# Moving the decay factors of a chunked attention: a masked table made on the chip, a scaled q on GpSimd, and xt evicted by ScalarE

## Chip, cores and metric

One Trainium2 chip, one core of it. The metric is device microseconds of one execution, a median over runs. Engines: PE is TensorE (PEld its weight loads), DVE is VectorE, ACT is ScalarE, POOL is GpSimd, SP is SyncE, which only issues transfers here. A "q" behind an engine's name means its issuing side.

## What is computed

Attention with a decay per head, then two mixtures of experts (MoE), one behind the other, the second with a limit of tokens for each expert.

```python
# q, k, v: 2 x 8 heads x 768 x 64
gamma = 1.0 - 2.0 ** (-5.0 - np.arange(H))
for t in range(S):
    state = gamma[None, :, None, None] * state + np.einsum('bhd,bhe->bhde', k[:, :, t], v[:, :, t])
    y[:, :, t] = scale * np.einsum('bhd,bhde->bhe', q[:, :, t], state)
...
x = y.transpose(0, 2, 1, 3).reshape(B * S, H * D)      # 1536 x 512
# each MoE layer, 8 experts, F = 1024
logits = x @ w_gate
expert_idx = np.argmax(logits, axis=1)
out[mask] = gate_w[mask, None] * (np.maximum(xe @ w1[e], 0.0) @ w2[e])   # xe = x[mask], for each expert e
```

Layer 2 keeps at most `capacity` tokens for each expert, in their order.

## The kernel before

The 1536 tokens are 12 tiles of 128, numbered n; tile n is chunk n // 2 of the sequence n % 2. The loop over n in `fused` (lines 662 to 700) does the attention chunk by chunk, in a software pipeline: step n holds the scores of tile n, the rest of tile n−1 and the combination of tile n−2. Each engine works through its own instructions in the order in which the code issues them; waits between engines are semaphores. What a step issues, in this order, with the letters that stand in the rows:

- `a_scores(n)`: on PE the products sc of k and q (line 508); on DVE two products Am = sc × mask (line 510), which cut off later positions.
- `a_decay(n+1)`: vp, the values times a power of gamma by position (line 498), on POOL (on DVE for tile 1).
- `combine` for tile n−2 (`comb(n−2)`): cb on PE (line 1334), which turns xt so that tokens lie on partitions, and adds the logits; DVE sums the logits (lgb or row, line 1340), ACT copies the row (lines 1345, 1349) and issues its store to x1d in HBM (line 564).
- `a_past(n−1)`: q times the state of the earlier chunks, on PE into ot (line 542).
- `a_state(n)`: du on PE (line 524), wn = du + state on DVE (line 527), wm = wn times gamma to the 128 on POOL (line 529).
- `a_out(n−1)`: Am times vp on PE, added to ot (line 555); DVE evicts it as xt = ot × g, in two halves (line 557). g holds the scale and the power of gamma of the query's position.
- the transfers of tile n+3 (qb, kt, vk) on SP's queue, and for n under 7 a clearing store of x2d.

The scale by position is thus split: vp carries gamma to the (127 − s) for the key, g carries gamma to the (s − 127) for the query, and both the chunk's own scores and the past go through g at the end.

The routing of the first eight tiles goes in two batches of four, started at n = 5 and n = 9. `pick` finds the best expert (bm, bk, bmk, boh, lines 588 to 592), `rank` counts on PE and DVE, and `slots` builds tables bR of 128x256 (line 622) that `place` feeds to PE (line 630). At n = 10 an early gather of rows from x1d is issued by POOL (rows<-x1d,eig, line 347). The last four tiles are routed one by one (rR line 234, tbp line 243). Behind the loop stand the end of tile 11, products h with the first expert's weights (`ahead`, line 434), and layer 1 and layer 2.

Weights arrive as f32 pieces st (line 138) and are split into two parts: whi by ACT (`split_hi`, line 159) and wlo by DVE (`split_lo`, line 170); the first expert's first four pieces (whole, line 150) are used as they are.

The constants lie in one table cst of 1236 columns. It is loaded in three pieces, of 320, 228 and 70 KB, among the first tiles on SP's queue (lines 638, 640, 697). PE opens with 40 products warm on ones (line 464), which compute nothing that is used.

Of the kernel before, what the change touches and what calls it, by code (L numbers as in the profile page):

```python
# [10 lines left out]
F32 = mybir.dt.float32  # L11
# [7 lines left out]
P = 128  # L19
# [3 lines left out]
NT = N // P  # L23
# [11 lines left out]
WARM = 40  # L35
# [10 lines left out]
def _consts(capacity):  # L46
    gamma = 1.0 - 2.0 ** (-5.0 - np.arange(H, dtype=np.float64))
    s = np.arange(P, dtype=np.float64)
    parts = []

    def put(name, a):
        a = np.asarray(a, dtype=np.float32).reshape(P, -1)
        lo = sum(x.shape[1] for x in parts)
        _C[name] = (lo, lo + a.shape[1])
        parts.append(a)

    put("mask", (s[:, None] <= s[None, :]))
    put("dec", gamma[None, :] ** (127.0 - s[:, None]))
    hh = np.array([[2 * p + j for p in range(NP)] for j in range(2)]).repeat(HD, axis=0)
    put("g128", gamma[hh] ** 128.0)  # L60
    ho = np.array([[4 * a + 2 * u + j for j in range(2) for a in range(2)] for u in range(2)]).repeat(HD, axis=0)
    put("g", (1.0 / np.sqrt(HD)) * gamma[ho][:, :, None] ** (s[None, None, :] - 127.0))
    put("ident", np.eye(P))
    put("lt", (s[:, None] < s[None, :]))
    put("rev", np.broadcast_to(8.0 - np.arange(E), (P, E)))
    put("iota", np.broadcast_to(np.arange(C0), (P, C0)))
    put("tok", P * np.arange(NT)[None, :] + s[:, None])
    put("tie", np.broadcast_to((E - np.arange(E)) / 16, (P, E)))
    put("pos", np.broadcast_to(np.arange(E), (P, E)))
    put("slot", np.stack([s, s + P], axis=1))  # L70
    put("caps", np.broadcast_to(np.minimum(np.array(CAPS), [[N], [capacity]]).reshape(1, -1), (P, 2 * E)))
    put("held", np.broadcast_to(np.array(CAPS[1]), (P, E)))
    cand = np.arange(P) // NM
    put("cj", cand[:, None] == np.arange(E)[None, :])
    put("cbase", [[c[j] + (p % NM) * P if j < E else 2000 for c in CAPS] for p, j in enumerate(cand)])
    return np.ascontiguousarray(np.concatenate(parts, axis=1))


@with_exitstack
def fused(ctx, tc, qT, kT, vkr, wg, w11, w12, w21, w22, cst, out, capacity):  # L80
# [15 lines left out]
    c0, c1 = _C["g128"][1], _C["ident"][1]  # L96
# [9 lines left out]
    ident = con("ident")  # L106
# [364 lines left out]
    with tc.tile_pool(name="ap", bufs=3) as ap:  # L471
# [6 lines left out]
        st_, vps = {}, {}  # L478

        def a_load(n):  # L480
# [3 lines left out]
            qb = ap.tile([P, NP, P], F32, tag="qb", name="qb", bufs=4)  # L484
# [16 lines left out]
        def a_scores(n):  # L501
# [7 lines left out]
            for j in range(2):  # L509
                V.tensor_mul(Am[:, :, j, :], sc[j], con("mask").unsqueeze(1).to_broadcast([P, NP, P]))  # L510
# [22 lines left out]
        def a_past(n):  # L533
            c, b = divmod(n, B)
            qb = ld.pop(n)[0]
# [10 lines left out]
        def a_out(n, beside=None):  # L546
# [4 lines left out]
            for j in range(2):  # L551
                for a in range(2):
                    for u in range(2):
# [3 lines left out]
                V.tensor_mul(xt[:, 2 * j:2 * j + 2], ot[j],  # L557
                             con("g").rearrange("p (k t) -> p k t", k=KD)[:, 2 * j:2 * j + 2])
# [96 lines left out]
        first, second = (hi + 1 for _, hi in BATCHES)  # L655
        a_decay(0)
# [6 lines left out]
        for n in range(NT):  # L663
            a_scores(n)
            if n == NT - 1:
                split_lo()
# [26 lines left out]
            if n == 0:  # L693
# [185 lines left out]
    def layer(li, xd, rin):  # L879
# [29 lines left out]
        if li == 0:  # L909
            ix = finish_route(rin, li, [None, None, lambda: evac(0), None, None, done])  # L910
# [517 lines left out]
```

## Time and profile before

| | us |
|---|---|
| median of 3 runs | 422.79 (421.86 to 422.96) |
| the profiled execution: time | 423.04 |
| the profiled execution: span in the trace | 421.3 |
| PE busy in the span | 408.0 (97%) |
| DVE busy | 319.4 (76%) |
| ACT busy | 238.6 (57%) |
| POOL busy | 98.1 (23%) |

The busy times are sums over the whole span, and the stages differ: the attention takes roughly the first 62 us, the rest are the MoE layers. The rows below come from the windows (busy time in a stretch), from the timeline (each instruction or group with what ended the idle time ahead of it) and from the chain that ended last.

### The profile page before, as it was taken

To read this page: it belongs to the slowest core of one execution; us is meant where nothing else is said; L and a number is where in the kernel's file an instruction comes from. 1 tells how busy PE (TensorE), PEld (TensorE's weight loads), DVE (VectorE), ACT (ScalarE), POOL (GpSimd) and SP (SyncE) were. 2 spreads that over 40 slices of the span, in tenths; PEclk is the share of its full clock that TensorE was granted. 3 is DMA by queue.
4 is the path that set the end of the run, shared out by engine and by line. 5 is a ranking of instruction groups with operands and counts; after the bars stand their busy time and mean duration, and the time that the engine had idled before them with its cause. 6 is when DMAs were issued, how large, how long until landed. Compare 5 with 4: busy or idle time off the path is not lost.

```text
span 421.3 us, 9473 instructions
## 1 busy us (share of the span) xinstructions
PE 408.0 (97%) x3403; PEld 382.0 (91%) x3403; DVE 319.4 (76%) x870; ACT 238.6 (57%) x485; POOL 98.1 (23%) x89
## 2 busy tenths in 40 slices
PE   8998989999999999999999999999999999999993
PEld 7887779999899999999999988999888999999993
DVE  3778787678989798989798867378576788887840
ACT  2111132567677676767665631557776678787650
POOL 2344313303023130404000204003221504021021
PEclk9999999999999999999999999999999999999999
DMA  8999983976667766767657903768867777778711
GB/s 309 397 389 385 344 325 99 345 262 206 237 222 232 242 211 235 237 226 233 225 178 222 330 10 78 308 220 269 293 219 256 229 247 261 243 240 269 233 42 33
DMA packets 32503, 100.45 MB, mean 238 GB/s; under 512 B 4669, under 2 KB 5181, under 8 KB 32448
## 3 DMA queue, kind: packets, MB, share of 16 engines
q1 hardware_dynamic: 25488, 82.74, 57.5%
q0 software_dynamic: 4656, 13.00, 9.0%
q10 hardware_dynamic: 2304, 4.02, 2.6%
q8 instruction: 29, 0.48, 0.4%
q14 instruction: 26, 0.21, 0.2%
HBM read 87.01 MB, written 12.99 MB: 237 GB/s over the span
## 4 chain that ended last, share of the span: by engine, by line
PE 74%; DMA 11%; DVE 6%; issue 3%; ACT 2%; SPq 1%; POOL 1%; POOLq 0%; ACTq 0%; DVEq 0%
PE h L800 16%; PE y L844 16%; PE h L801 7%; PE y L845 7%; PE h L434 5%; DMA st<-w 5%; PE cb L1334 4%; DMA vk<-vkr 3%; PE o L859 3%; PE o L861 3%; PE o L860 3%; PE tp L362 2%; DVE wlo L170 2%; DMA whole<-w 2%; DMA x1d<-row 1%
## 5 line engine op out<-in xcount | busy, mean ns | idle before, releaser
L170 DVE TENSOR_TENSOR wlo<-st,whi 128x1024 fp32r<-128x1024 f32 x120 | 145.0, 1216 | 2.5 <-ACT whi L159 2.5
L159 ACT CAST whi<-st 128x1024 fp32r<-128x1024 f32 x120 | 125.1, 1045 | 29.0 <-DMA st<-w 28.6
L844 PE MATMUL y<-h,whi 128*128 128x416 f32 (+9 forms) x384 | 117.2, 369 | 0.0
L800 PE MATMUL h<-x,whi 128*128 128x416 f32 (+9 forms) x384 | 114.5, 365 | 0.0
L845 PE MATMUL y<-h,wlo 128*128 128x208 f32 (+9 forms) x384 | 96.9, 252 | 0.0
L801 PE MATMUL h<-x,wlo 128*128 128x208 f32 (+9 forms) x384 | 96.7, 252 | 0.0
L844 PEld LDWEIGHTS y<-h,whi 128*128 128x128 f32 x384 | 72.1, 188 | 2.9 <-DVE rro L232 0.6
L800 PEld LDWEIGHTS h<-x,whi 128*128 128x128 f32 x384 | 72.1, 188 | 2.1 <-issue 0.6
L801 PEld LDWEIGHTS h<-x,wlo 128*128 128x128 f32 x384 | 73.4, 191 | 0.1
L845 PEld LDWEIGHTS y<-h,wlo 128*128 128x128 f32 x384 | 73.3, 191 | 0.0
L321 POOL DMA_INDIRECT x2d<-row,is x16 | 17.1, 1071 | 118.5 <-ACT row L1347 88.7
L812 DVE SCALAR_TENSOR_TENSOR h<-hs,h 128x416 fp32r<-128x416 f32 (+9 forms) x48 | 26.9, 561 | 19.1 <-ACT h L811 18.5
L321 POOL DMA_INDIRECT out<-ob,is x14 | 14.9, 1068 | 110.8 <-ACT ob L865 108.4
L811 ACT ACTIVATE h<-hs 128x416 fp32r<-128x416 f32 (+9 forms) x48 | 25.1, 523 | 25.5 <-DVE hs L786 25.4
L786 DVE TENSOR_TENSOR hs<-h,hb 128x208 f32<-128x208 f32 (+9 forms) x96 | 29.6, 347 | 6.8 <-ACT hb L785 6.8
L434 PE MATMUL h<-x,whole 128*128 128x128 f32 (+1 forms) x256 | 30.5, 277 | 0.0
L785 ACT COPY hb<-h 128x208 f32<-128x208 f32 (+9 forms) x96 | 27.0, 318 | 5.9 <-PE h L801 5.8
L1345 ACT COPY row<-cb 128x512 f32<-128x512 f32 x11 | 6.5, 586 | 41.1 <-DVE lgb L1340 25.0
L434 PEld LDWEIGHTS h<-x,whole 128*128 128x128 f32 x256 | 29.3, 192 | 0.3 <-issue 0.2
L347 POOL DMA_INDIRECT rows<-x1d,igs x14 | 24.3, 1735 | 9.2 <-issue 4.7
L786 DVE TENSOR_TENSOR yt<-y,yb 128x208 f32<-128x208 f32 (+9 forms) x48 | 15.0, 352 | 14.2 <-ACT yb L785 14.2
L859 PE MATMUL o<-whi,h 128*128 128x512 f32 (+1 forms) x64 | 24.3, 379 | 0.0
(198 smaller groups left out, 613.6 us busy)
## 6 DMA issues: line engine op xcount, KB each, us to landing
st<-w SPq DMA_DIRECT2D x120, 512.0 KB, 4.3
vk<-vkr SPq DMA_DIRECT2D x11, 512.0 KB, 6.0
whole<-w SPq DMA_DIRECT2D x8, 512.0 KB, 7.1
x2d<-zero SPq DMA_DIRECT2D x12, 260.0 KB, 7.6
qb<-qT SPq DMA_DIRECT2D x12, 256.0 KB, 5.7
x1d<-row ACTq DMA_DIRECT2D x11, 260.0 KB, 5.8
kt<-kT SPq DMA_DIRECT2D x11, 256.0 KB, 5.7
vk<-vkr ACTq DMA_DIRECT2D x1, 512.0 KB, 4.6
```

The source lines that it names most:

```text
L159: A.copy(hi, st)
L170: V.tensor_sub(lo, st, hi)
L321: ins = nc.gpsimd.indirect_dma_start(dst.rearrange("n (i d) -> (n i) d", i=parts) if parts > 1 else dst[:, :], bass.IndirectOffsetOnAxis(a ...
L434: T.matmul(ps[:, j], w[:, k, j % 2 * P:(j % 2 + 1) * P], x[:, k], start=k == 0, stop=k == KD - 1, skip_group_check=True)
L785: A.copy(b, ps[:, 1, :])
L786: V.tensor_add(out, ps[:, 0, :], b)
L800: T.matmul(ps, hi[:, k, fs], x[:, k, :, :cap], start=k == 0, stop=False, skip_group_check=True)
L801: T.matmul(ps[:, 0, :], lo[:, k, fs], x[:, k, 0, :cap], start=False, stop=k == KD - 1, skip_group_check=True)
L812: V.scalar_tensor_tensor(h[:, sl, 1, :cap], s, 0.0, h[:, sl, 0, :cap], ALU.max, ALU.subtract)
L844: T.matmul(ps[i], hi[:, ds], h[:, f, :, :cap], start=f == 0, stop=False, skip_group_check=True)
L845: T.matmul(ps[i][:, 0, :], lo[:, ds], h[:, f, 0, :cap], start=False, stop=f == KF - 1, skip_group_check=True)
L859: T.matmul(p, h[:, f, 0, ts_], hi, start=f == 0, stop=False)
```

## The change

- Scores: the mask becomes a table m8 of two halves (one for each j, the head's place in its pair), mask times the query's power of gamma and the scale. Am = sc × m8, in two DVE products of the same size as before.
- Past: from chunk 1 on, POOL makes qg = qb × gq, 128x512, right behind `a_scores(n)` in the code and ahead of vp(n+1); `a_past` reads qg in qb's place.
- xt therefore needs no factor, and ACT copies it from PSUM (two halves of 128x256); DVE's product goes.
- The tables: a new input grow of 2x896 (7 KB) is loaded first on ACT's queue; three products gb on PE (2 rows against 128x512) spread its powers over the partitions; DVE multiplies two of them with the mask into m8, ACT copies the third to gq. They stand in the code ahead of the first scores (`a_factors`).
- mask, ident, lt and iota are made by POOL at the start (three selects and an iota), and cst shrinks to 84 columns, one load of 42 KB. DVE's casts of lt and iota go.
- 24 warm-up products instead of 40; qb in three buffers instead of four.
- The `split_lo` at the last step of the loop and the two `split_hi` at the last but one leave the attention; the two `split_hi` move into the routing of layer 1, and the `split` behind it does one wlo more.

```diff
-WARM = 40
+WARM = 24
...
-    put("mask", (s[:, None] <= s[None, :]))
...
-    put("g", (1.0 / np.sqrt(HD)) * gamma[ho][:, :, None] ** (s[None, None, :] - 127.0))
-    put("ident", np.eye(P))
-    put("lt", (s[:, None] < s[None, :]))
...
-    put("iota", np.broadcast_to(np.arange(C0), (P, C0)))
...
+def _grow():
+    gamma = 1.0 - 2.0 ** (-5.0 - np.arange(H, dtype=np.float64))
+    h = 2 * np.arange(NP)[None, :] + np.arange(2)[:, None]
+    left = (1.0 / np.sqrt(HD)) * gamma[h][:, :, None] ** (np.arange(P) - 127.0)
+    j = np.arange(2)[:, None]
+    picks = [np.broadcast_to(j == 0, (2, P)), np.broadcast_to(j == 1, (2, P)), j == np.arange(P)[None, :] // HD]
+    return np.ascontiguousarray(np.concatenate([left.reshape(2, -1)] + picks, axis=1).astype(np.float32))
...
+        nc.scalar.dma_start(gr, grow)
+        mask = ap.tile([P, NP, P], F32, tag="xt", name="mask", bufs=2)[:, 0, :]
+        for t, op in (mask, ALU.is_ge), (ident, ALU.is_equal), (lt16, ALU.is_gt):
+            G.affine_select(t, ones16, pattern=[[1, P]], compare_op=op, fill=0.0, base=0, channel_multiplier=-1)
+        G.iota(iota16, pattern=[[1, C0]], base=0, channel_multiplier=0, allow_small_or_imprecise_dtypes=True)
...
+        def a_factors():
+            for j in range(3):
+                gb = mmtile("gb")
+                at = (NP + j) * P
+                T.matmul(gb, gr[:, at:at + P], gr[:, 0:NP * P], start=True, stop=True)
+                if j < 2:
+                    V.tensor_mul(m8[:, j], gb.rearrange("p (a t) -> p a t", a=NP),
+                                 mask.unsqueeze(1).to_broadcast([P, NP, P]))
+                else:
+                    A.copy(gq, gb.rearrange("p (a t) -> p a t", a=NP))
+
+        def a_query(n):
+            if n // B:
+                qg = ap.tile([P, NP, P], F32, tag="qg", name="qg", bufs=2)
+                G.tensor_mul(qg, ld[n][0], gq)
+                qgs[n] = qg
...
-            qb = ap.tile([P, NP, P], F32, tag="qb", name="qb", bufs=4)
+            qb = ap.tile([P, NP, P], F32, tag="qb", name="qb", bufs=3)
...
-                V.tensor_mul(Am[:, :, j, :], sc[j], con("mask").unsqueeze(1).to_broadcast([P, NP, P]))
+                V.tensor_mul(Am[:, :, j, :], sc[j], m8[:, j])
...
-            qb = ld.pop(n)[0]
+            ld.pop(n)
+            qb = qgs.pop(n, None)
...
-                V.tensor_mul(xt[:, 2 * j:2 * j + 2], ot[j],
-                             con("g").rearrange("p (k t) -> p k t", k=KD)[:, 2 * j:2 * j + 2])
+                A.copy(xt[:, 2 * j:2 * j + 2], ot[j])
...
-        nc.sync.dma_start(cs[:, :c0], cst[:, :c0])
+        nc.sync.dma_start(cs, cst)
         a_load(1)
-        nc.sync.dma_start(cs[:, c0:c1], cst[:, c0:c1])
...
+        a_factors()
         a_decay(0)
...
             a_scores(n)
-            if n == NT - 1:
-                split_lo()
+            a_query(n)
             a_decay(n + 1)
...
-                nc.sync.dma_start(cs[:, c1:], cst[:, c1:])
-            if n == 2:
-                V.tensor_copy(lt16, con("lt"))
-                V.tensor_copy(iota16, con("iota"))
...
-            if n == NT - 2:
-                split_hi()
-                split_hi()
...
-            ix = finish_route(rin, li, [None, None, lambda: evac(0), None, None, done])
+            ix = finish_route(rin, li, [None, None, lambda: evac(0), split_hi, split_hi, done])
```

PE, from the last warm-up on, before (line, operation, output <- inputs, shape, and how many in a row):

```order
L464 MATMUL warm<-ones_78 128x128
L508 MATMUL sc<-qb,kt 128x128 x8
L524 MATMUL du<-vp,vk 64x64 x8
L508 MATMUL sc<-qb,kt 128x128 x8
L524 MATMUL du<-vp,vk 64x64 x8
L555 MATMUL ot<-Am,vp 64x128 x8
```

and after:

```order
L466 MATMUL warm<-ones_79 128x128
L494 MATMUL gb<-gr 128x512 x3
L535 MATMUL sc<-qb,kt 128x128 x8
L551 MATMUL du<-vp,vk 64x64 x8
L535 MATMUL sc<-qb,kt 128x128 x8
L551 MATMUL du<-vp,vk 64x64 x8
L583 MATMUL ot<-Am,vp 64x128 x8
```

The three products gb stand ahead of the first scores; what follows keeps its order.

POOL, from the last tiles of the attention to the early gather (eig are its row numbers), before:

```order
L498 TENSOR_TENSOR vp<-vk,cs 128x512
L529 TENSOR_TENSOR wm_734<-wn_732,cs 128x256
L498 TENSOR_TENSOR vp<-vk,cs 128x512
L529 TENSOR_TENSOR wm_834<-wn_832,cs 128x256
L498 TENSOR_TENSOR vp<-vk,cs 128x512
L347 DMA rows<-x1d,eig 128x520
L347 DMA rows<-x1d,ig_1186 112x520
```

and after:

```order
L556 TENSOR_TENSOR wm_747<-wn_745,cs 128x256
L504 TENSOR_TENSOR qg<-qb,gq 128x512
L525 TENSOR_TENSOR vp<-vk,cs 128x512
L556 TENSOR_TENSOR wm_849<-wn_847,cs 128x256
L504 TENSOR_TENSOR qg<-qb,gq 128x512
L525 TENSOR_TENSOR vp<-vk,cs 128x512
L349 DMA rows<-x1d,eig 128x520
L504 TENSOR_TENSOR qg<-qb,gq 128x512
L349 DMA rows<-x1d,ig_1199 112x520
```

A qg stands ahead of each vp, and the last one, for tile 11, behind the early gather.

DVE, behind the first batch's count (n = 7), before:

```order
L1340 TENSOR_REDUCE lgb<-cb 128x8
L611 TENSOR_TENSOR E_122<-boh,cs 128x32
L613 TENSOR_TENSOR bro<-brk,boh 128x32
L614 TENSOR_REDUCE r_123<-bro 128x4
L527 TENSOR_TENSOR wn_576<-du,wm_427 128x256
L622 TENSOR_SCALAR bR<-iota_79,r_123 128x256 x2
L557 TENSOR_TENSOR xt<-ot,cs 128x256 x2
L510 TENSOR_TENSOR Am<-sc,cs 128x4x128 x2
```

and after:

```order
L1359 TENSOR_REDUCE lgb<-cb 128x8
L638 TENSOR_TENSOR E_107<-boh,cs 128x32
L640 TENSOR_TENSOR bro<-brk,boh 128x32
L641 TENSOR_REDUCE r_108<-bro 128x4
L554 TENSOR_TENSOR wn_585<-du,wm_432 128x256
L649 TENSOR_SCALAR bR<-iota_80,r_108 128x256 x2
L537 TENSOR_TENSOR Am<-sc,m_133 128x4x128 x2
```

xt is gone from the row; it stands on ACT, behind the row copies and the store of the tile before.

## Rows read from the trace of the kernel before

**Rows 1.** Windows: stretch, length, busy (count) PE PEld DVE ACT POOL, clock, DMA, GB/s.

```profile
30.00:40.00 10.00, 8.51 (x147) 7.20 (x146) 9.32 (x31) 1.37 (x4) 3.27 (x4) 1.00 1.03 386
...
60.00:70.00 10.00, 9.40 (x90) 8.78 (x89) 7.75 (x51) 2.58 (x6) 1.00 (x1) 1.00 0.27 88
...
100.00:200.00 100.00, 99.99 (x720) 96.62 (x719) 90.01 (x255) 70.21 (x145) 27.65 (x19) 1.00 0.68 227
```

**Rows 2.** Timeline, opening: start, us, engine, line, operation, out<-in, shapes, count, [idle before <-releaser].

```profile
1.07 4.45 PE L464 MATMUL warm<-ones 128*128 128x128 f16 x40 [1.07 <-DVE ones L461]
...
5.45 1.59 PE L508 MATMUL sc<-qb,kt 64*128 64x128 f32 x16
...
5.87 1.04 POOL L498 TENSOR_TENSOR vp<-vk,cs 128x512 f32<-128x512 f32 x1 [5.41 <-DMA vk<-vkr]
...
7.59 1.16 PE L508 MATMUL sc<-qb,kt 64*128 64x128 f32 x16
...
8.65 0.69 DVE L498 TENSOR_TENSOR vp<-vk,cs 128x512 f32<-128x512 f32 x1 [0.28 <-DMA vk<-vkr]
```

**Rows 3.** Timeline, PE behind the attention: prices of products at the high clock.

```profile
70.50 1.50 PE L374 MATMUL tp<-ones 128*128 128x128 f16 x24
...
72.23 8.20 PE L434 MATMUL h<-x,whole 128*128 128x128 f32 x72
```

**Rows 4.** Chain that ended last, tiles 2 and 3: start, us, what, count.

```profile
8.70 7.86 DMA vk<-vkr
...
17.81 0.69 PE du L524 x16
18.50 0.88 PE ot L555 x16
19.37 1.09 PE sc L508 x16
20.46 1.12 PE cb L1334 x8
21.59 0.60 PE ot L542 x16
```

**Rows 5.** DMA view, 0 to 100: loads of constants, size, us from issue to landing.

```profile
cs<-cst SPq DMA_DIRECT2D x1, 320.0 KB, 5.0
...
cs<-cst SPq DMA_DIRECT2D x1, 228.0 KB, 6.0
```

**Rows 6.** Timeline, tiles 7 and 8: slot tables on DVE and PE's waits.

```profile
32.48 1.60 DVE L622 TENSOR_SCALAR bR<-iota,r 128x256 f16<-128x256 f16 x2
...
34.56 1.17 PE L1334 MATMUL cb<-iw,xt 128*128 128x136 f32 x8 [1.00 <-DVE xt L557]
...
39.51 1.17 PE L1334 MATMUL cb<-iw,xt 128*128 128x136 f32 x8 [0.49 <-DVE xt L557]
```

**Rows 7.** Timeline, DVE in the picks of the first and second batch.

```profile
28.58 0.68 DVE L589 TENSOR_TENSOR bk<-lgb,bm 128x32 f32<-128x32 f32 x1
...
47.96 0.19 DVE L589 TENSOR_TENSOR bk<-lgb,bm 128x32 f32<-128x32 f32 x1
...
48.63 0.85 DVE L592 TENSOR_TENSOR boh<-bk,bmk 128x32 f16<-128x32 f32 x1
```

**Rows 8.** Timeline, end of the attention: the early gather, and PE's wait for rR.

```profile
55.12 1.22 POOL L347 DMA_INDIRECT rows<-x1d,eig  x1 [5.69 <-DMA whole<-w]
...
58.10 0.20 PE L243 MATMUL tbp<-E,rR 128*128 128x8 f16 x2 [1.14 <-DVE rR L234]
```

**Rows 9.** Timeline, ACT: a row's last copy, its store's issue, a half-size copy.

```profile
26.70 0.20 ACT L1349 COPY row<-lgb 128x8 f32<-128x8 f32 x1
...
28.09 0.33 ACTq L564 DMA_DIRECT2D x1d<-row  x1
...
63.74 0.37 ACT L1379 COPY row<-cb 128x256 f32<-128x256 f32 x1 [0.40 <-DVE lg L1370]
```

**Rows 10.** Timeline, DVE's splits of weights behind the routing.

```profile
73.81 2.36 DVE L170 TENSOR_TENSOR wlo<-st,whi 128x1024 fp32r<-128x1024 f32 x2 [1.17 <-ACT whi L159]
```

More of the change, by code (lines that the diff above doesn't have):

```diff
@@ L60, in _consts @@
     put("g128", gamma[hh] ** 128.0)
-    ho = np.array([[4 * a + 2 * u + j for j in range(2) for a in range(2)] for u in range(2)]).repeat(HD, axis=0)
-    put("g", (1.0 / np.sqrt(HD)) * gamma[ho][:, :, None] ** (s[None, None, :] - 127.0))
-    put("ident", np.eye(P))
-    put("lt", (s[:, None] < s[None, :]))
     put("rev", np.broadcast_to(8.0 - np.arange(E), (P, E)))
-    put("iota", np.broadcast_to(np.arange(C0), (P, C0)))
     put("tok", P * np.arange(NT)[None, :] + s[:, None])
@@ L76, in _consts, with fused @@
     return np.ascontiguousarray(np.concatenate(parts, axis=1))
+def _grow():
[5 more added lines that the diff above has]
+    return np.ascontiguousarray(np.concatenate([left.reshape(2, -1)] + picks, axis=1).astype(np.float32))
 @with_exitstack
-def fused(ctx, tc, qT, kT, vkr, wg, w11, w12, w21, w22, cst, out, capacity):
+def fused(ctx, tc, qT, kT, vkr, wg, w11, w12, w21, w22, cst, grow, out, capacity):
     nc = tc.nc
@@ L95, in fused @@
     cs = cp.tile([P, cst.shape[1]], F32, name="cs")
-    c0, c1 = _C["g128"][1], _C["ident"][1]
     def con(name):
@@ L104, in fused @@
     wgs = cp.tile([P, 2, KD, E], F32, name="wgs")
-    ident = con("ident")
+    ident = cp.tile([P, P], F32, name="ident")
     lt16 = cp.tile([P, P], F16, name="lt16")
@@ L477, in fused @@
         ld = {}
-        st_, vps = {}, {}
+        st_, vps, qgs = {}, {}, {}
+        gr = ap.tile([P, NP, 2, P], F32, tag="Am", name="gr", bufs=2).rearrange("p a j t -> p (a j t)")[0:2, 0:(NP + 3) * P]
+        nc.scalar.dma_start(gr, grow)
[3 more added lines that the diff above has]
+        G.iota(iota16, pattern=[[1, C0]], base=0, channel_multiplier=0, allow_small_or_imprecise_dtypes=True)
+        m8 = ap.tile([P, 2, NP, P], F32, name="m8", bufs=1)
+        gq = ap.tile([P, NP, P], F32, name="gq", bufs=1)
+        def a_factors():
[13 more added lines that the diff above has]
+                qgs[n] = qg
         def a_load(n):
@@ L1416 @@
         "w21": t1(np.asarray(inputs["moe2_w1"])), "w22": t2(np.asarray(inputs["moe2_w2"])),
-        "cst": _consts(capacity),
+        "cst": _consts(capacity), "grow": _grow(),
     }
```

## The prediction, made before the changed kernel ran

> **What bounds the kernel now.** I read the windows first. TensorE (PE) is busy 99.99 of the 100 us from 100 to 200 [rows 1]: the two MoE layers are a fixed amount of matmul work. The edits lie ahead of that, in the attention (up to about 62 us) and in the routing behind it, so what they gain or lose there is carried to the end at its own size, unless something else is late at the hand-over. In the attention PE is not full: 8.51 of 10 us in 30 to 40, and 9.40 in 60 to 70 [rows 1]. These stretches and the first 18 us are where time can move.
>
> Second, the opening in the timeline: 40 warm-up matmuls from 1.07, 4.45 long, then the first scores sc(0), which take 1.59 where the next sc takes 1.16; GpSimd (POOL) begins its first vp at 5.87, after 5.41 idle that end with vk's arrival [rows 2]. The warm-ups take 4.45 ÷ 40 = 0.111 each, later matmuls of the same shape 1.50 ÷ 24 = 0.0625 [rows 3]. So although the clock column says 1.00, the durations say that TensorE opens at its lower level (1.2 GHz). It rises within sc(0): half pace for x us costs x/2, so 1.59 − 1.16 = 0.43 is 0.86 us of it, and the rise is at 5.45 + 0.86 = 6.3.
>
> Third, the chain of waits: the transfer of vk(3) ends at 8.70 + 7.86 = 16.56, vp follows, and du(3) starts at 17.81; from there PE's own rows follow one another [rows 4] and nothing else is late until the routing of the first batch.
>
> **Part 1, the opening (tables worked out by three products).** 24 warm-ups end at 1.07 + 24 × 0.111 = 3.7. Then three products gb (2 rows against 128x512 f32) stand ahead of sc(0). An f32 record of 128 columns takes 8.20 ÷ 72 = 0.114 at the high level [rows 3]; gb has four times the columns and two records, so 3 × 2 × 4 × 0.114 = 2.7 us, or 5.4 at the lower level. If the clock rises at 6.3 as it did, 2.6 us pass at half pace (1.3 of the work) and 1.4 are left: gb ends and sc(0) starts at 7.7 instead of 5.45. From sc(0) to du(3) PE has 4 sc, 3 du, 2 out, 2 cb and one past: 4 × 1.09 + 3 × 0.69 + 2 × 0.88 + 2 × 1.12 + 0.60 = 11.0 [rows 4]; before, 17.81 − 5.45 = 12.4 passed, the rest being the slow sc(0) and waits for vk. Those waits go: the loads of 320 and 228 KB no longer stand ahead of vk(3) [rows 5], and 561 kB at 386 GB/s [rows 1] are 1.45 us, so vk(3) lands at 15.1 and its vp ends at 16.2. du(3) comes at 7.7 + 11.0 = 18.7: **+0.9**. Bounds: with a rise at 4.7 gb ends at 6.9, and du(3) at 17.95 with 0.05 of hand-overs, +0.1; with one only after gb, at 9.1, du(3) is at 20.1, +2.3. On POOL, mask, ident, lt and iota now stand ahead of vp(0). No row shows such an operation; the nearest is vp, 1.04 [rows 2], with four times the columns of a mask: between nothing and 4 × 1.04 = 4.2, under 5.41 of idle time either way, so I take nothing. DVE's two products with the mask, as long as Am's, lie under gb and sc(0).
>
> **Part 2, tiles 7 and 8.** VectorE (DVE) was late there: it worked through the slot tables bR (1.60 for two) and only then xt, and PE's cb waited 1.00 and 0.49 for xt [rows 6]. xt now goes to ScalarE (ACT), which copies 128x256 in 0.37 [rows 9], two a tile, under the next sc (1.09): −1.49. Against it stands POOL's new qg, 128x512 like vp, so 1.04 each, ten of them. DVE's operations that read SBUF alone stretch while POOL has such an operation: bk took 0.68 at 28.58, beside a vp, and 0.19 at 47.96, with POOL idle; boh took 0.85 beside a vp [rows 7]. A hold is thus 0.5 to 0.66 of DVE's time. bR is already held once; with two POOL operations a tile I charge one more, +0.55. Part 2: **−0.95** (bounds −1.5, and 0, where three holds eat it).
>
> **Part 3, picking the second batch (tile 9).** This DVE chain (bk to boh) lies ahead of Am and out on the path; one hold is in it already [rows 7]. qg(9) runs just ahead of that vp, beside the first of these operations. It starts before they do, so I charge less than a whole hold of 0.5: **+0.4**; bounds 0 and +1.04, all of qg.
>
> **Part 4, the end of the attention.** A wlo and both xt leave DVE's queue ahead of the slot table rR, and PE's wait of 1.14 for it goes [rows 8]: tbp would start at 58.10 − 1.14 = 56.95 and past(11) right behind, at 57.1, where it was at 58.25. But past(11) now needs qg(11), which POOL does behind the issue of the early gather: 55.12 + 1.22 + 1.04 = 57.4. So −0.85. Of the 0.60 that PE idles in 60 to 70 [rows 1], 0.45 is waiting behind xt and ranks on DVE and goes. Part 4: **−1.3**, bounds −1.6 (qg in time) and −0.25 (qg behind one more operation of 1.04).
>
> A rule of the Trainium skill speaks against qg on POOL. vp took 1.04 on POOL and 0.69 on DVE [rows 2], 1.5 times. The Trainium skill's "GPSIMD Engine Reference", section "Engine selection", gives elementwise two-input work to VectorE and calls GpSimd about twice as slow. By it qg would take 2 × 0.69 = 1.38 (an estimate), ten of them 3.4 us more of POOL's time and qg(11) 0.34 later, which turns the sum below into −0.4. The trace's ratio is milder, and the sum goes by the trace.
>
> **Part 5, behind the attention.** The split of one weight piece moves from the attention into the first routing: two whi on ACT and one wlo more on DVE, where four now stand in a row. DVE idled 1.17 ahead of the last two of them, waiting for whi, and one takes 2.36 ÷ 2 = 1.18 [rows 10]: the gap takes it, and what follows keeps its time. **+0.2** for hand-overs; bounds 0 and +1.2, a wlo that finds no gap.
>
> At nothing: the casts of lt and iota that go (DVE waits for PE there, at tile 2); the three loads of constants that become one of 42 KB, beyond the 1.45 us above; qb in three buffers instead of four, whose load now waits for sc(n) and qg(n) of the same step, both done before SP comes to it, and if POOL were late by an operation, the load of two tiles ahead would be by as much, which du doesn't see.
>
> Sum: 0.9 − 0.95 + 0.4 − 1.3 + 0.2 = **−0.75**. The profiled execution took 423.04 us (span 421.3), 0.25 above the median of 422.79: 422.3 for it and **422.0** for the median. A measurement of this kernel can tell about 0.3% (1.27 us) from no change: below 421.5 is faster, above 424.1 slower.
>
> **The rivals.** A, the clock; slower. The warm-up is cut before the rise and followed by products that use 2 of 128 rows. If TensorE doesn't rise with these, but only once full work has run for a while, say at 12, gb ends at 9.1, and the 2.9 us from there do 1.45 of work: du(3) is 3.8 late instead of 0.9, and the time is 422.0 + 2.9 = 424.9. From a rise at 10.5 on it is slower. For it: only dense 128-row matmuls preceded the rise here. Against: at the rise itself sc ran, which uses 64 rows [rows 2], and PE has no more gaps now than then.
>
> B, POOL's additions hold nobody; faster. qg may fall where DVE reads PSUM (Am, wn, tbp); the stretched rows read SBUF alone [rows 7]. Then part 2 is −1.5, part 3 nothing and qg(11) in time: 0.9 − 1.5 − 1.6 + 0.2 = −2.0, or 420.8; with the early rise of part 1, 420.0. Against it: with two POOL operations a tile a hold finds DVE's routing twice as often.
>
> C, ACT's queue. xt stands behind the issue of the x1d store, and that issue came at 28.09 although its row was ready at 26.70 + 0.20 [rows 9]: it waits 1.2 for an older transfer. xt has about 0.7 to spare under sc. Where the store waits so long, cb comes 0.5 late; in three tiles that is 1.5: 423.5.
>
> D, POOL opens late. If the first of the masks takes long, vp(0), du(0) and Am(0) are late. du(0) is itself 2.25 later now, so the cover is 5.41 + 2.25 = 7.7; 2 us beyond it give 422.0 + 2 = 424.0. The Trainium skill's "GPSIMD Engine Reference", section "Instruction dispatch", has the first call of a freshly loaded kernel pay for code loading, about 6 us; no run here shows it.
>
> **How the numbers follow.** Forecast 0.42 (421.1 to 423.2), A 0.15, B 0.25, C 0.08, D 0.10. Faster: B but for 0.02, and a third of the forecast's chance, 0.37. Slower: A from 10.5 on, 0.11, and the far ends of C and D, 0.07: 0.18. Within 0.3%: the rest, 0.45. The range of 420.2 to 424.3 leaves out 0.1 of B and 0.1 of A and D.
>
> **What would show it.** In the profile of the changed kernel: sc(0) at 7.7 and du(3) at 18.7 (A: sc rows near 2 us long, beyond 9); cb of tiles 7 and 8 with no wait; bk and boh stretched beside qg and vp; past(11) near 57.4, released by qg; vp(0) soon after vk(0) lands, at 5.9 (D: later than 7.7). I am wrong if PE waits for ACT's xt, or if PE stands idle around 72 or 97, because then gains ahead of it don't carry.

## The result and the profile after

The changed kernel took 426.03 us (median of 4 runs, 424.28 to 426.21), the kernel before 422.33 in the runs beside it: a ratio of 1.0095 [1.0069, 1.0122]. It is slower by 3.7 us, where 422.0 was forecast and the range ended at 424.3.

The profile that belongs to this result is of the 424.28 execution, 1.8 below the other three. Its page says (span, then busy time and count by engine):

```profile
span 422.5 us, 9477 instructions
...
PE 410.3 (97%) x3393; PEld 382.9 (91%) x3393; DVE 314.6 (74%) x846; ACT 247.9 (59%) x510; POOL 110.0 (26%) x103
```

DVE gave up 5 us, ACT took 9 and POOL 12, as the change says. PE is 2 us busier than before, 410.3 to 408.0. Where those lie, the timeline of the opening tells (start, us, engine, line, operation, count, [idle before <-releaser]):

```profile
1.14 2.74 PE L466 MATMUL warm<-ones 128*128 128x128 f16 x24 [1.14 <-DVE ones L463]
...
3.81 2.84 PE L494 MATMUL gb<-gr 2*128 2x512 f32 x6
...
6.58 1.55 PE L535 MATMUL sc<-qb,kt 64*128 64x128 f32 x16
...
8.91 1.04 POOL L525 TENSOR_TENSOR vp<-vk,cs 128x512 f32<-128x512 f32 x1 [6.65 <-DMA vk<-vkr]
...
10.01 1.12 PE L551 MATMUL du<-vp,vk 128*64 128x64 f32 x16 [1.88 <-POOL vp L525]
...
11.06 2.08 PE L535 MATMUL sc<-qb,kt 64*128 64x128 f32 x16
```

and the windows of PE there (stretch, length, busy, granted clock, DMA share, GB/s):

```profile
6.00:7.00 1.00, 1.00 (x8) 1.00 0.98 324
7.00:8.00 1.00, 1.00 (x14) 0.60 0.93 337
8.00:9.00 1.00, 0.13 (x2) 0.50 1.04 406
...
13.00:14.00 1.00, 1.00 (x20) 0.50 0.86 215
14.00:15.00 1.00, 1.00 (x21) 0.99 0.99 389
```

gb ran at the high level (2.84, where 2.7 was worked out for it), then the clock was granted at half from about 7.2 to 14.0, from the middle of sc(0) on. vk(0) landed 3 us later than before, so PE idled 1.88 ahead of du(0). sc(1) takes 2.08, where the row of before that answers to it has 1.16 [rows 2]. From 15 on nothing of this is left, and the loss of the opening is made. du(3) is at 21.60, where it was at 17.81 [rows 4].

Two further profiles of the same kernel, taken later (below, again2 and again3), took another course. This is the opening of again2, an execution of 425.92:

```profile
3.81 5.48 PE L494 MATMUL gb<-gr 2*128 2x512 f32 x6
...
9.22 2.08 PE L535 MATMUL sc<-qb,kt 64*128 64x128 f32 x16
11.22 1.12 PE L551 MATMUL du<-vp,vk 128*64 128x64 f32 x16
12.28 2.08 PE L535 MATMUL sc<-qb,kt 64*128 64x128 f32 x16
...
14.29 1.12 PE L551 MATMUL du<-vp,vk 128*64 128x64 f32 x16
15.19 1.23 PE L583 MATMUL ot<-Am,vp 128*64 128x128 f32 x16
16.35 1.26 PE L535 MATMUL sc<-qb,kt 64*128 64x128 f32 x16
```

Here the lower level lasts from the warm-ups through gb (5.48, twice 2.7), two rounds of scores and du(1), until about 15; the clock column says 1.00 all that time, as it did over the slow warm-ups of the kernel before, so only the durations show it. This is rival A.

Start times of the same groups on PE show where each part of the change went. Each is the start in the timeline, in us; "last ob" is ACT's last eviction of layer 2.

| | before | before2 | after | again | again2 | again3 |
|---|---|---|---|---|---|---|
| time of the execution | 423.04 | 422.97 | 424.28 | 422.96 | 425.92 | 424.99 |
| sc(0) | 5.45 | 5.13 | 6.58 | 6.82 | 9.22 | 9.22 |
| sc(4) | 19.30 | 19.88 | 23.09 | 20.70 | 24.46 | 23.07 |
| sc(6) | 27.91 | 28.48 | 31.70 | 29.31 | 33.07 | 31.96 |
| sc(9) | 42.98 | 43.09 | 45.19 | 42.99 | 46.57 | 45.46 |
| sc(11) | 52.75 | 52.73 | 55.48 | 53.29 | 56.86 | 55.77 |
| first h | 63.78 | 64.39 | 65.62 | 63.93 | 67.46 | 66.51 |
| h x72 | 72.23 | 72.84 | 74.49 | 72.82 | 76.34 | 75.39 |
| last ob | 414.26 | 413.62 | 416.21 | 415.09 | 418.06 | 416.70 |

For again2 against before: +5.16 up to sc(4), −1.05 from there to h x72 (51.88 instead of 52.93), −0.31 from h x72 to the last ob, +3.80 in all; what follows the last ob took 0.9 less, and the span is 2.9 longer. The opening lost 1.4 to 5.2 in the four profiles of the changed kernel, and from sc(4) to h x72 each of them was 0.6 to 1.5 shorter than the kernel before. Two things stand against calling that a gain of the change. A late opening alone does the same: before_gb below, which has none of the rest of the change, took 51.86 from sc(4) to h x72, as again2 did (51.88). And from h x72 to the last ob the two profiles of the kernel before differ by 1.25 (342.03 and 340.78; the changed kernel 341.31 to 342.27), so that a difference of 1 cannot be followed to the end.

### The profile page after: what moved, and what is told of

It is laid out like the page before. It is cut to its first block, busy times and chain, and to the rows that moved or that the text cites. A ratio compares the mean times of both kernels' runs of the same rounds, so it can differ in the third digit from the quotient of the medians.

```text
span 422.5 us, 9477 instructions
## 1 busy us (share of the span) xinstructions
PE 410.3 (97%) x3393; PEld 382.9 (91%) x3393; DVE 314.6 (74%) x846; ACT 247.9 (59%) x510; POOL 110.0 (26%) x103
## 4 chain that ended last, share of the span: by engine, by line
PE 92%; DVE 2%; issue 2%; DMA 2%; POOL 1%; ACTq 0%; POOLq 0%; ACT 0%; DVEq 0%
PE y L863 19%; PE h L819 18%; PE y L864 8%; PE h L820 8%; PE h L436 6%; PE cb L1353 6%; PE sc L535 3%; PE o L878 3%; PE o L880 3%; PE o L879 3%; PE tp L364 3%; PE ot L583 2%; PE du L551 2%; DMA vk<-vkr 2%; PE ot L570 1%
## 5 line engine op out<-in xcount | busy, mean ns | idle before, releaser
L831 DVE SCALAR_TENSOR_TENSOR h<-hs,h 128x416 fp32r<-128x416 f32 (+9 forms) x48 | 26.9, 561 | 19.3 <-ACT h L830 18.7
L878 PE MATMUL o<-whi,h 128*128 128x512 f32 (+1 forms) x64 | 24.3, 379 | 0.0
L880 PE MATMUL o<-whi,h 128*128 128x512 f32 (+1 forms) x64 | 23.5, 366 | 0.0
```

Of the source, the lines that this page charges most:

```text
L878: T.matmul(p, h[:, f, 0, ts_], hi, start=f == 0, stop=False)
L880: T.matmul(p, h[:, f, 1, ts_], hi, start=False, stop=f == KF - 1)
```

## The experiments

Each is the changed kernel with the edit shown, unless it says otherwise. Ratios are to the kernel before, run beside it.

**again, again2, again3**: no edit.

> The changed kernel once more, for a second profile of its opening. In the first one vk(0), whose issue stood behind gr and kt(0) on ScalarE's queue, landed at 8.8 instead of 5.8, PE idled 1.88 ahead of du(0), and the clock was granted at half from 7.2 to 14.0; du(3) came at 21.6, 3.8 later than before. Theory Q (queue): the late landing is a result of the order of the loads and comes again, with du(0) at about 10. Theory C (chance): it was one execution's, and vk(0) lands near 6 here; then du(0) follows sc(0) at about 8.1. Both: 424 to 426.5.

> The changed kernel again, for one more profile: both profiled executions so far (424.28 and 422.96) were its fast ones, while most of its times lie near 426.2. Theory A: in the usual execution the clock stays at half through gb and the first scores, as in vk0_on_sp and before_gb: gb 5.4 to 5.5 long, sc(0) at 9.2, sc(4) at 23.3 to 23.7, time 426. Rival F (it rises ahead of gb and falls behind it, as in the two profiles): gb 2.8 to 3.1, half clock from 7.2 on, time 423 to 424.5, and then the 426 comes from elsewhere (a fall near 58 to 62).

> As again2, a further profile of the same kernel: theory A gives gb of 5.4 to 5.5 us and sc(4) at 23.3 to 23.7 with 426; rival F gives gb of 2.8 to 3.1 and a half clock behind it.

again: 426.62, ratio 1.0075 [1.0055, 1.0096]; its profiled execution took 422.96. vp(0) began at 6.67 there, when vk(0) had landed, and PE did not wait ahead of du(0), so the 1.88 of idle time was one execution's: theory C. The clock fell behind gb again (half from 7.7 to 11.2), and sc(4) was 1.4 late. again2 (425.92) and again3 (424.99) both show gb at 5.48 and sc(0) at 9.22: theory A. In both, vk(0) was in time for du(0). So the late rise goes with the two profiles that lie nearer the usual time, and the fall behind gb with the two shorter executions; four profiles are too few to say how often each comes, and none of them is of an execution of 426.0 to 426.9, where six executions without a profile lie. Their mean granted clock is 0.993 to 0.996, that of again2 0.997, and that of the two with a fall behind gb 0.989 and 0.991: this speaks for the late rise in them, but does not show it (again3 has 0.991 for a fall at 58).

**before2**: the kernel before.

> The kernel before, for a second profile of its opening. If its opening depends on chance as the changed kernel's does, the first scores take 1.1 to 2.1 and sc(4) comes between 19.0 and 20.5; the clock does not fall behind sc(0), since no work with few rows stands there. Time 420 to 424.

422.97. sc(0) took 1.16 from 5.13 on, sc(4) came at 19.88. With the scores right behind 40 warm-ups the opening moves by 0.6 between the two profiles, not by 4.

**vk0_on_sp**

```diff
-            (nc.scalar if n == 0 else nc.sync).dma_start(vk, vkr[b, c])
+            nc.sync.dma_start(vk, vkr[b, c])
```

> The changed kernel with one edit: vk(0) is issued by SP right behind qb(0), not by ScalarE behind gr and kt(0). Theory Q: vk(0) lands at about 5.5, du(0) follows sc(0) at 8.1 without the 1.9 of idle time. If the low clock came from that idle time, du(3) is at 19.2 or earlier and the time 2 to 2.5 below the changed kernel's. Theory G (the low clock follows the three 2-row products, whatever comes behind them): the clock is at half from about 7 again, du(3) at 20 or later and the gain at most 1.9. If vk(0) was not what PE waited for, no change.

426.27, 1.0081 [1.0063, 1.0098]. vk(0)'s product vp(0) ran at 5.97, but gb took 5.48, sc(0) stood at 9.22 and sc(4) at 23.62. The transfer was not what the time hung on: with vk(0) early the kernel lost as much.

**warm40**

```diff
-WARM = 24
+WARM = 40
```

> The changed kernel with 40 warm-up products as before instead of 24. The warm-ups then end at 4 to 5.5, gb at 7 to 8.2, sc(0) starts there, 1 to 1.6 later than in the changed kernel, and du(0) still waits for vk(0) at about 10. Theory G: the clock falls behind gb as it did, for as long: du(3) at 21.6 to 23, time equal to the changed kernel's or up to 1.5 more. Theory W (too short a warm-up lets the clock fall): no half clock behind gb, du(3) at 19.6 to 20, 2 less than the changed kernel.

426.14, 1.0071 [1.0046, 1.0097]. The profile has the rise inside the warm-ups (40 took 3.65), gb at the high level but for its end (3.07), and then the fall: half clock from 7.2 to 14.0, sc(0), sc(1) 2.08 each, sc(4) at 23.06. The clock was high ahead of gb and fell all the same. Theory W falls.

**before_gb**: the kernel before, with grow loaded, 24 warm-ups and the three products.

```diff
-WARM = 40
+WARM = 24
...
+        for j in range(3):
+            gb = mmtile("gb")
+            at = (NP + j) * P
+            T.matmul(gb, gr[:, at:at + P], gr[:, 0:NP * P], start=True, stop=True)
         a_decay(0)
```

> The kernel before with one part of the change alone: grow loaded, 24 warm-ups and the three products gb ahead of sc(0), their results unused. Theory R: the clock rises late or falls behind gb, sc(4) comes 2.5 to 4 later than in the kernel before (at 21.8 to 23.3 instead of 19.3), and the time is 2.5 to 4 more. My first sum (gb costs its duration, and the clock rises as before): sc(4) at 20.2, +0.9.

425.80, 1.0103 [1.0044, 1.0162]: this one part alone costs what the whole change costs. It takes the 24 warm-ups along; no run has them without the products, but with 40 (warm40) the loss was the same. Its opening in the timeline:

```profile
3.74 5.49 PE L670 MATMUL gb<-gr 2*128 2x512 f32 x6
...
9.15 2.08 PE L519 MATMUL sc<-qb,kt 64*128 64x128 f32 x16
11.16 1.12 PE L535 MATMUL du<-vp,vk 128*64 128x64 f32 x16
12.21 1.67 PE L519 MATMUL sc<-qb,kt 64*128 64x128 f32 x16
```

sc(4) came at 23.31, 4.0 later than before, not 0.9. From there to h x72 it took 51.86, the kernel before 52.93: PE's waits for xt in tiles 7 and 8 were nothing and 0.22, although VectorE still evicts xt. The kernel before first, then before_gb:

```profile
32.39 1.04 POOL L498 TENSOR_TENSOR vp<-vk,cs 128x512 f32<-128x512 f32 x1 [2.60 <-DMA vk<-vkr]
...
35.05 1.04 POOL L509 TENSOR_TENSOR vp<-vk,cs 128x512 f32<-128x512 f32 x1 [2.70 <-PE brk L620]
...
36.07 0.86 DVE L633 TENSOR_SCALAR bR<-iota,r 128x256 f16<-128x256 f16 x2
...
37.51 1.19 PE L1349 MATMUL cb<-iw,xt 128*128 128x136 f32 x8
...
42.21 1.17 PE L1349 MATMUL cb<-iw,xt 128*128 128x136 f32 x8 [0.22 <-DVE xt L568]
```

In the kernel before, vp waited for vk's transfer and ran beside bR [rows 6]. In before_gb, where PE is later, vp no longer waits for the transfer and ends as bR begins.

**rows128**: vk0_on_sp, and grow padded with zeros to 128 rows, so that gb uses all rows at the same columns.

```diff
-    return np.ascontiguousarray(np.concatenate([left.reshape(2, -1)] + picks, axis=1).astype(np.float32))
+    a = np.concatenate([left.reshape(2, -1)] + picks, axis=1).astype(np.float32)
+    return np.ascontiguousarray(np.concatenate([a, np.zeros((P - 2, a.shape[1]), np.float32)]))
```

> vk0_on_sp with the three products gb over 128 rows: grow is padded with 126 rows of zeros (458 KB instead of 7), the same results at the same number of columns. Theory R (products that use 2 of 128 rows do not raise the clock, or let it fall): with 128 rows gb runs at or reaches the high level, no half clock behind it, sc(0) at 6.8 to 7.5, sc(4) at 20 to 20.8 instead of 23.6, and the time about 3 below vk0_on_sp, near 423. Theory L (any f32 product of 512 columns does it, whatever its rows): sc(4) at 23 or later, as in vk0_on_sp, and the time 426.

```profile
5.64 4.66 PE L495 MATMUL gb<-gr 128*128 128x512 f32 x6 [1.77 <-DMA gr<-grow]
...
10.23 1.16 PE L536 MATMUL sc<-qb,kt 64*128 64x128 f32 x16
```

With 128 rows the clock rose within gb (4.66 lies between 2.7 and 5.4), sc(0) ran at the high level, and no half clock came behind it. For the course of the clock in this profile that is theory R. The time did not follow, 425.96, 1.0082 [1.0048, 1.0117]: the load of 448 KB made gb wait 1.77, sc(0) stood at 10.23 and sc(4) at 23.00. As the course also differs between profiles of one kernel, one profile is a hint that the rows matter, and does not show it; as a remedy the experiment is none.

**gb_f16**: vk0_on_sp with grow as two f16 terms in 4 rows, one pass for each product, and 40 warm-ups.

```diff
+    hi = left.astype(np.float16)
+    lo = ((left - hi) * 4096).astype(np.float16)
+    rows = [np.concatenate([hi, picks], axis=1), np.concatenate([lo, picks / 4096], axis=1)]
```

> vk0_on_sp with grow in f16 (two terms, 4 rows) and 40 warm-ups: gb takes one pass of 512 columns for each product, 0.65 in all at the high level and 1.3 at the lower one, a quarter of the f32 products' time. Theory R with time (the clock falls because some 3 us or more of work with few rows stand in the opening): no half clock behind gb, sc(0) at 5.5 to 6.8, sc(4) at 18.8 to 19.8, and the time 2.0 to 1.2 below the kernel before, 421 to 421.8, since what follows sc(4) gains 1.5. If even so short a stretch lets the clock fall: sc(4) at 21 or later and 423 or more.

423.62, 1.0041 [1.0013, 1.0069]: 2.4 less than the changed kernel, still above the kernel before. gb took 0.82, no half clock followed, sc(4) came at 19.67. From there to h x72 it took 52.52, only 0.4 less than before; a wait of cb for xt in step 6 is new. The lines of ACT and PE there:

```profile
26.65 0.59 ACT L1368 COPY row<-cb 128x512 f32<-128x512 f32 x1 [1.23 <-DVE lgb L1363]
27.13 0.20 ACT L1372 COPY row<-lgb 128x8 f32<-128x8 f32 x1
...
29.58 0.33 ACTq L595 DMA_DIRECT2D x1d<-row  x1
29.95 0.65 ACT L589 COPY xt<-ot 128x256 f32<-128x256 f32 x2 [2.62 <-PE sc L539]
30.38 1.19 PE L1357 MATMUL cb<-iw,xt 128*128 128x136 f32 x8 [0.81 <-ACT xt L589]
```

The row was ready at 27.33, its store was issued at 29.58, and xt stood behind it: rival C, of which the changed kernel's own profiles show at most 0.21 (again3). Waits of 0.3 and more for ScalarE's xt are only in versions whose sc(4) comes by 21.1.

**gb_f16_q11**: gb_f16 with the last qg ahead of the early gather.

```diff
+                a_query(NT - 1)
                 early(rt1, x1d, nb * P)
```

> gb_f16 with the last qg (tile 11) moved ahead of the early gather on GpSimd, one tile earlier. In the changed kernel it ran from 58.51 to 59.79 and VectorE's E (1.17 instead of 0.22) was held beside it, so that PE waited 0.83 for rR. Theory H (the hold): E takes 0.22 again, past(11) comes 0.6 to 0.9 earlier against sc(11), and the first h 0.3 to 0.9 earlier; time 0.3 to 0.9 below gb_f16. Rival: the gather is issued 1.3 later, and its rows are late for tp: no gain, or a loss up to 0.5.

423.99, 1.0033 [0.9994, 1.0072], no gain. In the profile E took 0.22 again, as theory H has it, and PE waited neither for rR nor for the gather's rows, so the rival did not come. Yet sc(11) to the first h took 10.71, gb_f16 10.23: the clock was granted at half from 54.6 to 58.1, with PE busy all that time. The opening took another course too, though its work is that of gb_f16: gb took 1.46, sc(0) 2.08, and sc(4) came at 20.78. A late rise thus comes behind 40 warm-ups and 4-row f16 products as well.

**f32_behind**: 40 warm-ups, and the f32 products behind sc(0).

```diff
                     T.matmul(sc[j][:, p, :], kt[hs, p, :], qb[hs, p, :], start=True, stop=True)
+            if n == 0:
+                a_factors()
```

> The changed kernel with 40 warm-ups and the three f32 products gb behind sc(0) instead of ahead of it. Theory P (the place: whatever stands ahead of the scores while the clock is low costs up to twice, and the scores raise the clock): sc(0) at 4.8 to 5.5 as in the kernel before, sc(4) at 20 to 21 instead of 23.1. Theory R in full (2-row products let the clock fall wherever they stand): half clock behind gb again, sc(4) at 22 to 23.5, no gain.

In the profile (425.08) sc(0) came at 5.09, gb took 2.84, no half clock followed, sc(4) stood at 20.93: theory P for that execution. The time is 426.56, 1.0083 [1.0056, 1.011], and the mean granted clock of its other executions lies at 0.982 to 0.995, mostly below the 0.993 of the profiled one. What they did is not in a profile.

**f16_behind** (gb_f16 with the products behind sc(0)) and **store_behind** (that, with the store's issue behind the next xt):

```diff
-            a_store(n, row)
+            if n < NT - 2:
+                stores.append((n, row))
...
                 a_out(n - 1)
+            while stores:
+                a_store(*stores.pop(0))
```

> gb_f16 with the products gb behind sc(0): sc(0) follows the 40 warm-ups as in the kernel before and gb takes 0.65 to 1.3 there, under the wait for vp. sc(4) at 18.5 to 19.3 (19.30 before, 19.67 in gb_f16). What is left is then the x1d store: in gb_f16 its issue waited until 29.58 and xt stood behind it, so that cb waited 0.81. That wait comes here too, as large or larger (0.8 to 1.5), and the time stays within 0.5 of gb_f16 or 0.5 below it: 422.5 to 423.5.

> f16_behind with the issue of each x1d store moved on ScalarE's queue behind xt of the next tile. If the store's wait is what held xt and cb: no wait of cb for xt, sc(7) to sc(8) unchanged, the time 0.8 to 1.5 below f16_behind and 0.5 to 1.5 below the kernel before. Rival: the wait for the transfers only moves, to vk and so to vp and du, or the store comes late for the early gather: no gain over f16_behind.

424.72, 1.0027 [0.9991, 1.0063], and 426.02, 1.0063 [1.0041, 1.0086]. In f16_behind's profile the clock fell behind gb once more (0.50 from 9 to 11), though gb took only 0.82; sc(4) came at 21.08, not at 18.5 to 19.3. In store_behind cb no longer waits for xt, and sc(9) stands at 42.18, 0.8 earlier than in the kernel before. It loses at the end of the attention: rR stands beside qg and takes 2.24, and the clock falls behind the stretch where PE has gaps (columns as in rows 1):

```profile
56.06 2.24 DVE L240 TENSOR_SCALAR rR<-iota,r 128x256 f16<-128x256 f16 x1
56.93 1.27 POOL L508 TENSOR_TENSOR qg<-qb,gq 128x512 f32<-128x512 f32 x1
...
58.36 0.20 PE L249 MATMUL tbp<-E,rR 128*128 128x8 f16 x2 [1.84 <-DVE rR L240]
```

```profile
54.00:58.00 4.00, 2.51 (x41) 1.94 (x39) 3.91 (x10) 1.23 (x3) 2.32 (x2) 1.00 0.98 347
58.00:62.00 4.00, 3.64 (x34) 2.96 (x35) 1.79 (x11) 0.37 (x1) 0.21 (x1) 0.58 0.37 130
```

The same fall is in again3 (0.71 from 58 to 62), gb_f16_q11, xt_dve and qg_dve, and in neither profile of the kernel before.

**qg_dve**: store_behind with qg on VectorE.

```diff
-                G.tensor_mul(qg, ld[n][0], gq)
+                V.tensor_mul(qg, ld[n][0], gq)
```

> store_behind with qg made by VectorE (0.69 each, by vp's row) instead of GpSimd. Theory H (holds): the stretched rows beside qg go (bk 0.19 again where no vp runs), sc(10) to sc(11) shrinks from 5.98 by 0 to 0.5, and past(11) no longer waits behind a held E; against it stand 0.69 in each tile on VectorE, which shows in tiles 7, 9 and 11, where VectorE is late: net between 0.6 faster and 1.0 slower than store_behind. The rule that elementwise work of two inputs belongs on VectorE would give the fast end.

427.60, 1.0111 [1.0082, 1.0141]; the profiled execution took 422.68. In it sc(10) to sc(11) is 5.27 instead of 5.98: the hold of the second pick is gone (boh 0.19). But the early gather came late (tp waited 1.36 for its rows), and the clock fell from 62 on. In its profile the placing of qg is worth 0.7 of a tile. Three executions without a profile took 427.45 to 428.09, longer than any of store_behind's, at a mean granted clock of 0.982 to 0.987 where the profiled one has 0.992; what they did is not known.

**xt_dve**

```diff
-                A.copy(xt[:, 2 * j:2 * j + 2], ot[j])
+                V.tensor_copy(xt[:, 2 * j:2 * j + 2], ot[j])
```

> The changed kernel with xt copied by VectorE as before (without a factor), not by ScalarE. It measures parts 2 and 4 of the prediction. If moving xt is what took PE's waits of 1.00 and 0.49 in tiles 7 and 8 away, they come back, longer by a hold or two of the doubled GpSimd work: 1.5 to 2.5 slower than the changed kernel by sc(9), and another 0.5 to 0.8 at the end of the attention. If those waits went because of something else (slot tables earlier), the same time within 0.5.

426.95, 1.0086 [1.0061, 1.0111]. PE's waits for xt in tiles 7 and 8 came back, 0.66 and 0.22, and sc(4) to sc(11) took 34.19 instead of 32.39, +1.8. With qg on GpSimd, moving xt to ScalarE is worth that much there. The whole times (ratios 1.0086 and 1.0095) do not tell the two apart.

**tables_loaded**: 40 warm-ups, no products; m8 and gq come ready-made (512 and 256 KB).

```diff
+        nc.sync.dma_start(m8.rearrange("p j a t -> p (j a t)"), grow[:, 0:2 * NP * P])
         a_load(1)
+        nc.sync.dma_start(gq.rearrange("p a t -> p (a t)"), grow[:, 2 * NP * P:])
```

> The changed kernel without the products gb: m8 and gq are loaded ready-made (512 and 256 KB, where the kernel before loaded 320 and 228 KB), 40 warm-ups, the rest as changed. Theory O (the loss is the opening's, made by gb's place and rows): sc(0) at 5.1 to 5.5, no half clock behind it, 220 KB more than before are 0.6 us of transfers, so sc(4) at 19.5 to 20.3, and the 1.5 gained behind sc(4) is kept: the time is between 1.2 below and 0.3 above the kernel before. Rival S (the rest of the change loses too in most executions, by a clock that falls near the end of the attention or by stores on ScalarE's queue): 1 to 2.5 above it.

The profiled execution took 422.63, with sc(0) at 5.51 and no half clock; sc(4) came at 20.52, since sc(1) waited 1.09 for kt, and from sc(4) to h x72 it took 52.06 instead of 52.93. Over all its executions the median is 424.92, 1.0063 [1.004, 1.0087], so theory O holds for the opening and not for the time, which lies 2.7 above the kernel before, just beyond rival S's 1 to 2.5. cb waited 0.58 for xt behind a store in it too. Of the executions at 424 to 426 there is no profile.

## Why the prediction was wrong

**The step that failed** is in part 1: "If the clock rises at 6.3 as it did". The prediction carried the rise of the kernel before over to an opening with other work in it. The price by either level was right: gb took 2.84 and 5.48, where 2.7 and 5.4 were worked out. The course of the clock was not. It either stayed low until about 12 to 15 (again2, again3, vk0_on_sp, before_gb) or rose ahead of gb and fell behind it for 3 to 7 us (after, again, warm40). The part was put at +0.9, with +2.3 for its far end; measured at sc(4) it was +1.4 to +5.2, and before_gb shows +4.0 for it alone. The far end was wrong too: it let the clock be high from the end of gb, and in again2 sc(0), du(0), sc(1) and du(1) stood at half as well.

**Rival A** had this mechanism, with its point (a rise after 10.5 makes the kernel slower) and a price of 424.9 for a rise at 12. again3, with the rise in sc(1), had du(3) at 21.58, 3.8 late as rival A worked out, and took 424.99; again2, with a rise near 15, 425.92. It was given 0.15, because sc, which uses 64 rows, ran at the rise of the kernel before. That argument looked at the work at the moment of the rise, and not at the 4.45 us of 128-row products ahead of it. The range ended below both. That the few rows are what delays the rise is argued, not shown: rows128 is for it, and in f32_behind's profile the same 2-row products behind sc(0) went without a fall, so that the place may matter as well.

**The early landing of vk(3)**, −1.45 of transfers, did come: in again vp(3) ran at 14.86, before at 16.72. It was worth nothing, as PE was later than that in every profile.

**Part 2** came out larger than forecast, but not by its mechanism alone: sc(6) to sc(9) took 13.49 in the profile after, 15.07 before, −1.58, and −1.4 to −1.6 in the others; forecast −0.95. The lines of tiles 7 and 8, against [rows 6]:

```profile
36.04 0.86 DVE L649 TENSOR_SCALAR bR<-iota,r 128x256 f16<-128x256 f16 x2
...
36.78 1.27 POOL L504 TENSOR_TENSOR qg<-qb,gq 128x512 f32<-128x512 f32 x1
37.28 1.19 PE L1353 MATMUL cb<-iw,xt 128*128 128x136 f32 x8
...
41.69 1.19 PE L1353 MATMUL cb<-iw,xt 128*128 128x136 f32 x8
```

cb waits for nothing, and bR ran clear of POOL's operations, 0.86 instead of 1.60: the hold that I charged did not come, and the old one went too. Against before2, where the waits of cb were 1.0 together, the gain of this stretch is 1.1. But before_gb, with xt on VectorE and no qg, took 13.76: the late opening removes most of these waits by itself, and against it the rest of the change gains 0.3 here. Where the opening is earlier and no store holds xt, the gain stands: f32_behind (sc(4) at 20.93) and store_behind (20.07) took 13.50.

**Part 3** was right: sc(9) to sc(11) took 10.29, before 9.77, +0.5 for the +0.4. The rows that answer to [rows 7] are held beside qg and vp:

```profile
49.36 0.61 DVE L616 TENSOR_TENSOR bk<-lgb,bm 128x32 f32<-128x32 f32 x1
...
49.89 1.26 POOL L504 TENSOR_TENSOR qg<-qb,gq 128x512 f32<-128x512 f32 x1
50.01 1.19 DVE L617 TENSOR_TENSOR bk<-bk,cs 128x32 f32<-128x32 f32 x1
...
51.11 1.04 POOL L525 TENSOR_TENSOR vp<-vk,cs 128x512 f32<-128x512 f32 x1
...
51.45 0.75 DVE L619 TENSOR_TENSOR boh<-bk,bmk 128x32 f16<-128x32 f32 x1
```

**Part 4** had the wait of [rows 8] in the wrong place. past(11) did not wait for qg(11) but still for rR, since qg(11) held E on DVE:

```profile
58.51 1.28 POOL L504 TENSOR_TENSOR qg<-qb,gq 128x512 f32<-128x512 f32 x1
...
58.66 1.17 DVE L227 TENSOR_SCALAR E<-roh,cs 128x8 f16<-128x8 f16 x1
...
60.36 0.20 PE L245 MATMUL tbp<-E,rR 128*128 128x8 f16 x2 [0.83 <-DVE rR L236]
```

0.83 of the 1.14 are left (1.3 in again2). sc(11) to the first h took 10.14 to 10.74 instead of 11.03: −0.3 to −0.9, forecast −1.3 (before2 took 11.66). The 0.45 of idle time between 60 and 70 was misread: the timeline of before has two waits of 0.30 there, both put down to DMA:

```profile
61.63 0.63 PE L377 MATMUL tp<-cs,rows 128*128 128x128 f32 x4 [0.30 <-DMA rows<-x1d,eig]
...
63.68 0.20 PE L243 MATMUL tbp<-E,rR 128*128 128x8 f16 x2 [0.30 <-DMA x1d<-row]
```

In before2 the second is put down to rR. The changed kernel has a new one of 0.36, of cb for E. **Part 5**: the first h to h x72 took 8.87 instead of 8.45, +0.4 for the +0.2. That is not the moved split but a wait for the last tile's routing on DVE, which the kernel before has in neither profile:

```profile
67.14 0.17 PE L225 MATMUL rk<-roh,lt 128*128 128x8 f16 x1 [0.39 <-DVE roh L213]
```

Behind the start of h x72 some profiles have a second wait, and it is the prediction's own sign of being wrong, PE idle around 72. In again, ACT's copy x came 2.1 after the start of the products tp that it reads, where it came 0.4 after them in the profile after:

```profile
72.43 0.55 PE L379 MATMUL tp<-ident,rows 112*128 112x112 f32 x4
...
74.53 0.59 ACT L380 COPY x<-tp 128x224 f32<-128x224 f32 x2 [3.39 <-PE h L436]
...
74.93 7.40 PE L436 MATMUL h<-x,whole 128*128 128x112 f32 x64 [1.05 <-ACT x L380]
```

The same wait, 0.93 to 1.01, is in vk0_on_sp, warm40, xt_dve, f32_behind, f16_behind, store_behind and qg_dve, and in none of the three with the two `split_hi` where the kernel before has them (before, before2, before_gb). Seven profiles with the moved `split_hi` lack it too, so the move does not explain it by itself; what held ACT is not shown.

**The size of qg** was read off vp, at 1.04. It took 1.27: vp's second input is one column for each head, qg's is as long as the first. The Trainium skill's "GPSIMD Engine Reference", section "Engine selection", had given about 1.38 (an estimate) by twice VectorE's time; VectorE made the same qg in 0.68 in qg_dve, 1.27 is 1.9 times that, and the trace agrees with the page better than with the row that I took.

**Rival B** came in part 2 only (no hold at bR); DVE was held in parts 3 and 4. **Rival D** did not come: POOL's three selects and the iota took 0.28 to 0.34 each and were done at 2.3. **Rival C** is small in the changed kernel (0.21 in again3) and appears in versions with an earlier sc(4) (gb_f16 0.81, tables_loaded 0.58).

Open is why the kernels with a mended opening do not keep what the rest of the change gains. tables_loaded is the clearest: its profiled execution took 422.63, its median is 424.92. The mean granted clock is 0.999 in the profiled one and 0.988 to 0.995 in the six others, three of them below the 0.993 that is the lowest of the kernel before beside it, so the clock was lower in these. Several profiles of other versions show a second fall of the clock at the end of the attention; that it is this fall which makes the longer executions is not shown. None of the versions beats the kernel before.

## What to carry to other kernels

Work that is put into the opening has to be priced with the clock that it will meet, and the course of the clock has to be taken from a profile with that work in it, not from the one without: here 2.7 us of products with 2 rows ahead of the first scores made tile 4 start 4.0 later (before_gb). Where a gain hangs on such a course, several profiles are needed; the first profile of the changed kernel showed a late transfer and a fall of the clock behind the products, and the two last ones had neither. A gain behind a late opening has to be measured against a kernel that is as late and has nothing else of the change: here that comparison took most of it away. And an eviction that is moved to another engine stands behind everything that this engine issues, a store that waits for a transfer among it (0.81 in gb_f16).

## What was not expected of the hardware

- The clock fell in the middle of dense work: in warm40 it rose inside the 40 warm-ups, was high until near the end of gb, and half from 7.2 to 14.0, although PE had no gap up to 9.8 and 0.34 us of gaps in all. In rows128, with gb over 128 rows, it rose within gb and stayed.
- VectorE operations on SBUF data were held for nearly the whole of a GpSimd operation with two long inputs: rR, 0.29 by itself, took 2.24 beside a gather's issue and qg (store_behind); E took 1.17 instead of 0.22 beside qg (after).
- The same load landed more than 2 us apart in two executions of one kernel: vp(0), which waits for vk(0), began at 8.91 and at 6.67.
